# Infini-attention and GEGLU on one core: follow-up work placed by one table of step numbers, ten attention steps, last adds on VectorE

## The chip, the core and the metric

The kernel runs on one core of a Trainium2 chip. The metric is the device time of one execution in microseconds, as the median of several runs. The core has TensorE (PE) for matrix products, VectorE (DVE), ScalarE (ACT) and GpSimd (POOL) for the rest, SyncE (SP) which here only issues transfers, and 16 DMA engines. SBUF is the working memory, PSUM the memory that PE writes to.

## What is computed

The input x has 2048 rows of 448. It is layer-normed; the result xn goes through an attention with 16 heads of 28, and through a gated feed-forward of width 1792. The output is x + s * silu(b), s being the attention's result and b the feed-forward's.

```python
for s in range(4):                       # four segments of 512 rows
    qs, ks, vs = ...                     # 16 heads of 28
    p = softmax(qs @ ks.T * scale + causal mask)
    a_dot = p @ vs
    num, den = phi(qs) @ M, phi(qs) @ z + 1e-6    # phi(t) = t + 1 if t > 0 else exp(t)
    o = g * num / den + (1 - g) * a_dot           # g = sigmoid(beta), one per head
    M, z = M + phi(ks).T @ vs, z + sum(phi(ks))   # memory for the next segment
s = concat(o) @ wo
b = (gelu(xn @ w_gate) * (xn @ w_up)) @ w_down
out = x + s * silu(b)
```

## The kernel before

The work goes by the four segments. Each is held transposed (features on partitions, 512 rows along the free dimension), in four groups (G) of four heads, each head padded to 32 partitions. Two kinds of phases alternate on PE: gate 0, attention 0, gate 1, attention 1, gate 2, gate 3, attention 2, attention 3, tail. The order of instructions on every engine is the order in which the program calls them; nothing reorders them afterwards.

A **gate phase** (`gate_up`, L486) has 14 chunks. Each chunk takes eight matmuls (L496, and L503 on half the rows) into one of two PSUM buffers of `ps_s`; ACT applies GELU (L511), DVE multiplies gate by up (L512) and so frees the buffer. After every chunk the work that a table `steps` holds for this chunk number is called, then `tick()`.

An **attention phase** (`attention`, L577) has 12 steps: for each group the banks of `BANKS` (key block 0; key blocks 1 and 3 together; key block 2). A step makes the scores of four heads (L397, four matmuls side by side on 32 rows each) into both `ps_s` buffers, ACT takes the exponential of each (L403), GpSimd sets what lies above the diagonal to zero (L407), and two steps later PV (L418) sums into the one buffer of `ps_pv`. After a group's last bank `evac` (L426) copies the result to SBUF (L431) and sends its sums of weights, one row per head, by DMA to `dc` (L435). The PV of the last two steps is returned as two functions (`ends`) and called in the phase that follows. Between the steps stand fill units, in a merged order with an estimated cost each: projections of the next segment (`qk`, L314, cast at L318, then phi on ACT and DVE at L330, L337, L339; `v`, L352), the product with w_down (L523; tanh L526, L530) and the finish (L552, product L555, addition of x on GpSimd L559, store from GpSimd's queue L560). All of these use the three PSUM buffers of `ps_m`. `later(n, fn)` puts a function off by n ticks.

The **follow-up work** of a segment: `invert` (L444) turns the sums in `dc` into gate over sum, splits this into three bf16 terms and sends them by DMA to `rows`; a matmul with `spread` (L465) spreads them over the partitions of a group; `combine` (L472) scales the attention's result by them and adds the memory's. For the memory, `memory_read` (L439), an `invert` with side 1 and `scale_memory` (L468) do the same; `update` (L368) adds to M. Before, each of these is placed by hand: small tables made with `in_turn`, `tail` and `memory`, separately for each phase (L660 to L723).

`guard` (L204) checks on the chip that the weights are small enough for an exponential without a maximum: ACT squares wq and wk in four pieces, eight matmuls with a column of ones (L218) sum them, DVE does the rest. A second program (`general_path`) runs only if the check fails.

The **tail** finishes the w_down product of segment 3 (`d3[6:]`), runs the last two PV, inverts and combines group by group, and sums the product with wo in the freed `ps_s` buffers (L728). Then four output blocks go through two DVE or GpSimd operations each (L738, L740) to the output.

## Time and profile before

The median is 273.7 us (three runs, 271.87 to 273.88). The profiled execution took 273.37 us; its span in the trace is 271.6 us, all times below count from its start.

| engine | busy us | instructions |
|---|---|---|
| PE | 249.3 | 1630 |
| DVE | 190.0 | 371 |
| ACT | 155.5 | 226 |
| GpSimd | 100.2 | 203 |

| row of the page | operation | count, mean |
|---|---|---|
| L496, L503 | gate and up matmuls | 448, about 0.38 us each with overlap |
| L523 | w_down matmuls | 224 |
| L403 | exponential | 96, 885 ns |
| L407 | mask on GpSimd | 128, 449 ns |
| L512 | gate times up on DVE | 56, 685 ns |
| L559 | last add on GpSimd | 12, about 1.05 us |
| L560 | store issued from GpSimd | 12, 577 ns |
| L218 | sums of squares | 8, 352 ns |

The page's rows give, per line of the program, the busy time, the mean of one instruction and what ended the idle time before it. Matmuls overlap, so the distance between the starts of two of them is less than the duration of one. A timeline line gives the start, the time to the end of the group, the engine, line and tile, the number of instructions merged, and in brackets the idle time before it and what ended it.

### The profile page before, as it was taken

What the parts mean: (1) busy time and instruction counts of PE and PEld (TensorE: products, weight loads), DVE (VectorE), ACT (ScalarE), POOL (GpSimd) and SP (SyncE); (2) the same over time, 40 slices, a digit from 0 to 9 for tenths busy, and PEclk for the clock granted to TensorE, in tenths of its full rate; (3) what the DMA queues carried; (4) which work ended last, traced back from release to release, by engine and by line L of the source; (5) the groups of instructions that cost most, each with busy time, mean ns of one, the idle gap of its engine ahead of it and who ended that gap; (6) DMA issues with size and microseconds to landing.
All of it is one profiled execution on the core that took longest, in us unless ns stands there. A gap on an engine that the chain in (4) does not pass through costs nothing.

```text
span 271.6 us, 4546 instructions
## 1 busy us (share of the span) xinstructions
PE 249.3 (92%) x1630; PEld 104.5 (38%) x1630; DVE 190.0 (70%) x371; ACT 155.5 (57%) x226; POOL 100.2 (37%) x203
## 2 busy tenths in 40 slices
PE   7899999999999999999999999999899998995940
PEld 7543334433333335444434333344333333332410
DVE  5876977667686878577778646355878756876862
ACT  2546735788985335688963332625887687871100
POOL 2100410455521400966622205121776563658011
PEclk9999999999999999999999999999999999999795
DMA  7999026020110143101110310002000010001002
GB/s 221 393 277 213 0 41 154 12 23 19 23 22 6 34 85 113 22 18 39 40 37 0 63 24 0 4 6 72 18 21 21 5 29 8 4 1 57 19 7 75
DMA packets 26358, 15.11 MB, mean 56 GB/s; under 512 B 17880, under 2 KB 25048, under 8 KB 26328
## 3 DMA queue, kind: packets, MB, share of 16 engines
q1 hardware_dynamic: 23032, 9.96, 16.7%
q10 hardware_dynamic: 2720, 3.40, 3.9%
q0 software_dynamic: 576, 1.38, 1.5%
q8 instruction: 15, 0.25, 0.4%
q14 instruction: 15, 0.12, 0.2%
HBM read 9.18 MB, written 1.84 MB: 41 GB/s over the span
## 4 chain that ended last, share of the span: by engine, by line
PE 66%; DVE 16%; ACT 6%; DMA 5%; issue 3%; POOL 1%; SPq 1%; DVEq 0%; ACTq 0%
PE s L496 22%; PE m L523 11%; PE m L314 9%; PE s L503 5%; PE s L397 5%; PE m L352 4%; PE pv L418 3%; ACT pt L403 3%; PE m L465 2%; DMA x_sb<-in_A_x_dram 2%; PE m L552 2%; DVE hT L512 2%; DMA rows<-terms 2%; PE m L441 1%; DMA dc<-oU 1%
## 5 line engine op out<-in xcount | busy, mean ns | idle before, releaser
L403 ACT ACTIVATE pt<-s 128x1024 bf16<-128x1024 f32 (+1 forms) x96 | 79.2, 885 | 16.8 <-PE s L397 16.3
L407 POOL TENSOR_SCALAR_AFFINE_SELECT pt<-pt 128x256 bf16<-128x256 bf16 x128 | 54.6, 449 | 71.5 <-ACT pt L403 70.0
L511 ACT ACTIVATE gl<-s 128x512 bf16<-128x512 f32 x56 | 33.4, 597 | 55.5 <-PE s L496 28.7
L512 DVE TENSOR_TENSOR hT<-gl,s 128x512 bf16<-128x512 bf16 x56 | 38.4, 685 | 31.4 <-ACT gl L511 31.3
L523 PE MATMUL m<-wd_sb,hT 128*128 128x448 bf16 x224 | 52.3, 361 | 0.9 <-DVE wu_sb L470 0.9
L496 PE MATMUL s<-xnT,wg_sb 128*128 128x512 bf16 x168 | 45.7, 381 | 1.2 <-DVE hT L512 1.2
L496 PE MATMUL s<-xnT,wu_sb 128*128 128x512 bf16 x168 | 45.4, 379 | 0.0
L523 PEld LDWEIGHTS <-hT 128*128 128x128 bf16 x224 | 20.7, 99 | 23.6 <-issue 6.8
L496 PEld LDWEIGHTS <-wu_sb 128*128 128x128 bf16 x168 | 16.4, 98 | 19.8
L397 PE MATMUL s<-qT,kT 32*128 32x512 bf16 (+3 forms) x256 | 20.9, 301 | 2.6 <-ACT pt L403 2.3
L496 PEld LDWEIGHTS <-wg_sb 128*128 128x128 bf16 x168 | 14.1, 97 | 22.2 <-issue 9.7
L247 POOL TENSOR_TENSOR rstd<-rstd,nhalf 128x2 f32<-128x2 f32 x8 | 5.7, 712 | 45.7 <-DVE rstd L245 45.7
L503 PE MATMUL s<-xnT,wg_sb 64*128 64x512 bf16 x112 | 19.4, 384 | 0.4 <-DVE hT L512 0.4
L318 DVE CAST kT<-m 128x512 bf16<-128x512 f32 x16 | 11.0, 688 | 11.2 <-PE m L314 11.0
L418 PE MATMUL pv<-pt,vaug 128*32 128x512 bf16 (+3 forms) x256 | 17.3, 307 | 0.0
L314 PE MATMUL m<-xnT,wk_pad 128*128 128x512 bf16 x64 | 17.1, 380 | 0.0
L314 PE MATMUL m<-xnT,wq_pad 128*128 128x512 bf16 x64 | 16.8, 380 | 0.2 <-DVE vaug L354 0.2
L397 PEld LDWEIGHTS <-kT 32*128 32x128 bf16 x256 | 6.5, 91 | 23.4 <-issue 23.1
L526 ACT ACTIVATE th<-m 128x448 f32<-128x448 f32 x16 | 8.8, 548 | 11.3 <-PE m L523 11.1
L352 PE MATMUL m<-wv_sb,xnT 128*128 128x448 bf16 x64 | 14.1, 352 | 0.6 <-DVE wu_sb L431 0.3
L465 PE MATMUL m<-rows,spread 128*128 128x512 bf16 x28 | 11.0, 391 | 3.1 <-DMA rows<-terms 2.6
L431 DVE COPY oU<-pv 128x512 f32<-128x512 f32 x13 | 8.9, 688 | 4.8 <-PE pv L418 4.8
(102 smaller groups left out, 305.7 us busy)
## 6 DMA issues: line engine op xcount, KB each, us to landing
x_sb<-in_A_x_dram SPq DMA_DIRECT2D x7, 224.0 KB
wd_sb<-in_B_w_down_dram SPq DMA_DIRECT2D x1, 1568.0 KB
wg_sb<-in_B_w_gate_dram SPq DMA_DIRECT2D x1, 1344.0 KB
wu_sb<-in_B_w_up_dram ACTq DMA_DIRECT2D x1, 1344.0 KB
out_dram<-o_out POOLq DMA_DIRECT2D x12, 112.0 KB, 2.1
xr<-in_A_x_dram ACTq DMA_DIRECT2D x2, 448.0 KB
wo_sb<-in_A_wo_dram SPq DMA_DIRECT2D x4, 98.0 KB
dc<-oU SPq DMA_DIRECT2D x24, 8.0 KB
```

Source lines behind the costliest of these rows:

```text
L314: nc.tensor.matmul(out=pr[:], lhsT=wpad[nm][:, c, g * HG:(g + 1) * HG, :].rearrange("p h d -> p (h d)"), rhs=xnT[s][:, c, :], start=(c == ...
L352: nc.tensor.matmul(out=vp[:, 0:D], lhsT=xnT[s][:, c, b * P:(b + 1) * P], rhs=wv_sb[:, c, :], start=(c == 0), stop=(c == NDC - 1))
L397: nc.tensor.matmul(out=sp[i // 2][:, i % 2, c0:c0 + n], lhsT=kT[s][r, g, kb * P:(kb + 1) * P], rhs=qT[s][r, g, kb * P:L], start=True, stop ...
L403: nc.scalar.activation(out=pt[:, :, 0:w], in_=sp[pr][:, :, 0:w], func=ACT.Exp, scale=scale)
L407: nc.gpsimd.affine_select(out=v, in_=v, pattern=[[0, 2], [1, P]], compare_op=ALU.is_ge, fill=0.0, base=0, channel_multiplier=-1)
L418: nc.tensor.matmul(out=acc[i * HP:(i + 1) * HP, kb * P:L], lhsT=va[:, kb, g * HG + i, :], rhs=pts[i // 2][:, i % 2, c0:c0 + n], start=(kb ...
L465: nc.tensor.matmul(out=r[:], lhsT=spread[:, g, :], rhs=rows[side][:], start=True, stop=True)
L496: nc.tensor.matmul(out=gu[:, i, :], lhsT=w_sb[:, c, cols], rhs=xnT[s][:, c, :], start=start and c == 0, stop=stop and c == NDC - 2)
L503: nc.tensor.matmul(out=gu[:, i, :], lhsT=wg_sb[rs, NDC - 1, cols], rhs=xnT[s][rs, NDC - 1, :], start=start, stop=stop)
L511: nc.scalar.activation(out=gl[:], in_=gu[:, 0, :], func=ACT.Gelu_apprx_tanh)
L512: nc.vector.tensor_tensor(out=hT[s][:, fc, :], in0=gl[:], in1=gu[:, 1, :], op=ALU.mult)
L523: nc.tensor.matmul(out=d_ps[:, 0:D], lhsT=hT[s][:, fc, b * P:(b + 1) * P], rhs=wd_sb[:, fc, :], start=(fc == 0), stop=(fc == NFC - 1))
```

## The change

One dictionary, `PLAN`, now holds the step number of every piece of follow-up work. A single counter of slots runs through the whole program: 14 for each gate phase, 20 for each attention (two half steps for each of ten), then one for each unit of the tail. `put(name, fn)` files a function under its slot and asserts its order; `go()` is called once per slot and runs what is filed there. `merge` gives each list of fill units its own stretch of the phase (`"qk0": (0.609, 0.899)`), where it used to be the whole phase, or one of two parts of it.

Second, `STEPS` packs the key blocks of two groups into five steps, so that each step's exponential covers 512 columns for each head: block 2 of an odd group is computed with block 2 of the even group and kept until the odd group's accumulation has begun. `ptp` goes from 6 to 8 buffers, `pkp` from 3 to 2.

Third, the last add and its store go from GpSimd to DVE and SP; those of segment 2 write into `wq_pad`'s place. Three of segment 2's finish units move to the tail. The guard's squares are first added on GpSimd, so that two matmuls remain. `later` with 0 calls at once, the memory's product in `update` uses the buffers of `th`, and `follow` chooses the engine of the copies and inversions by phase. The aim is to keep PE supplied: fewer steps, fewer instructions on GpSimd, and each follow-up where its inputs are ready and its engine has room.

```diff
+PLAN = {
+    "stats10": 0, ..., "check0": 9, "check1": 3,
+    "check2": 8, "check3": 7, "check4": 13, "fill0": 9, "fill1": 1, "fill2": 18, "delay_phi": 2,
+    "delay_phi_end": 1, "delay_th": 0, "delay_sg": 2, "lead0": 2.29, "lead1": 1.56, "lead2": 2.93,
+    "lead3": 0.42, "upd0": (0.02, 0.233), "v0": (0.068, 0.299), "down0": (0.277, 1),
+    "qk0": (0.609, 0.899), "upd1": (0.072, 0.095), "v1": (0, 0.284), "down1": (0.319, 0.969),
+    "qk1": (0.122, 0.721), "fin1": (0.303, 1.05), "v2": (0.031, 1.05), "qk2": (0.082, 0.998),
+    "fin2": (0, 0.984), "down2": (0, 1.05), "split2": 8, "down3": (0.305, 1.05),
+    "fin3": (0.787, 1.05), "split3": 7, "fin_in": 1, "fin_at": 3, "end00": 34, "end01": 35,
+    "inv0": 36, ..., "inv2": 121,
+    "end30": 137, "end31": 137, "inv3": 138, "inv3l": 139, ..., "cmb30": 143, ..., "cmb31": 148,
+    ..., "cmb32": 150, ..., "scl32": 123, ..., "invm3": 112, "upd2": 89, "delay_out": 2, "check5": 17,
+}
...
-        ptp = pool("ptp", 6)
+        ptp = pool("ptp", 8)
...
-        pkp = pool("pkp", 3)
+        pkp = pool("pkp", 2)
...
+            for sq in sqs.values():
+                nc.gpsimd.tensor_tensor(out=sq[:, 0:2, :], in0=sq[:, 0:2, :], in1=sq[:, 2:4, :],
+                                        op=ALU.add)
+                nc.gpsimd.tensor_tensor(out=sq[:, 0, :], in0=sq[:, 0, :], in1=sq[:, 1, :], op=ALU.add)
...
-                for c in range(NDC):
-                    nc.tensor.matmul(out=np_[0:1, 0:D], lhsT=ones[:], rhs=sqs[nm][:, c, :],
-                                     start=(c == 0), stop=(c == NDC - 1))
+                nc.tensor.matmul(out=np_[0:1, 0:D], lhsT=ones[:], rhs=sqs[nm][:, 0, :],
+                                 start=True, stop=True)
...
-        BANKS = (((0, 0),), ((1, 0), (3, 384)), ((2, 0),))
+        STEPS = []
+        for a in range(0, G, 2):
+            b = a + 1
+            STEPS += [[(a, 0, 0)], [(a, 1, 0), (a, 3, 384)], [(a, 2, 0), (b, 2, 256)],
+                      [(b, 0, 0)], [(b, 1, 0), (b, 3, 384)]]
...
-                    nc.gpsimd.tensor_tensor(out=o_out[:], in0=t, in1=xr[s][:, b, :], op=ALU.add)
-                    nc.gpsimd.dma_start(out=o_v[s][:, b, :], in_=o_out[:])
-
-                later(99 if s == 2 else 1, rest)
+                    nc.vector.tensor_tensor(out=o_out, in0=t, in1=xr[s][:, b, :], op=ALU.add)
+                    nc.sync.dma_start(out=o_v[s][:, b, :], in_=o_out)
+
+                later(plan["delay_out"], rest)
...
-                    keyed.append(((c + u[0] / 2) / tot, n, u))
+                    keyed.append((a + (b - a) * (c + u[0] / 2) / tot, n, u))
...
+        def go():
+
+            for f in todo.pop(slot[0], ()):
+                f()
+            slot[0] += 1
...
+                    theirs.append((theirs or [lead])[-1] + 1.39)
...
-        ends = attention(3, d2[8:] + d3[:6] + finish_units(2), at, lead=0.6)
+        fin, w = finish_units(2), plan["fin_in"]
+        ends = attention(3, merge(3, down=d2[y:] + d3[:x], fin=fin[:w]))
+        gate_now[0] = True
+        follow(3, ends)
+        rest = d3[x:]
+        n = plan["fin_at"]
+        rest[n:n] = fin[w:]
+        for u in rest:
+            run([u])
+            go()
```

## The prediction

> **What bounds the kernel now.** I read the page's first part, then the windows cut by stage, then the timeline of one attention step and of the tail, and last the groups by form.
>
> ```profile
> PE 249.3 (92%) x1630; PEld 104.5 (38%) x1630; DVE 190.0 (70%) x371; ACT 155.5 (57%) x226; POOL 100.2 (37%) x203
> ```
>
> TensorE (PE) is the engine that is nearly always busy; so work taken off the others only counts where PE waits for it. The stages, by PE's own order: gate 0, attention 0, gate 1, attention 1, gates 2 and 3, attention 2, attention 3, the tail, the output.
>
> ```profile
> 24.20:45.60 21.40, 21.20 (x104) 8.21 (x104) 17.26 (x42) 9.92 (x15) 4.06 (x7) 1.00 0.34 57
> 45.60:76.20 30.60, 30.16 (x237) 12.72 (x236) 20.12 (x36) 26.05 (x38) 15.20 (x33) 1.00 0.18 34
> 76.20:103.40 27.20, 26.78 (x137) 10.04 (x135) 20.76 (x45) 12.63 (x22) 4.54 (x13) 1.00 0.24 47
> 103.40:136.00 32.60, 32.60 (x255) 14.19 (x254) 24.19 (x40) 26.25 (x36) 20.32 (x39) 1.00 0.15 39
> 136.00:187.10 51.10, 50.69 (x264) 20.00 (x263) 31.32 (x60) 20.96 (x35) 12.54 (x22) 1.00 0.09 18
> 187.10:217.00 29.90, 28.23 (x210) 10.87 (x208) 23.00 (x39) 24.06 (x31) 18.26 (x37) 1.00 0.10 30
> 217.00:243.00 26.00, 23.60 (x200) 9.23 (x200) 18.59 (x35) 21.04 (x28) 13.62 (x34) 1.00 0.05 11
> 243.00:262.50 19.50, 15.11 (x75) 6.25 (x75) 13.62 (x27) 2.47 (x5) 7.23 (x11) 0.91 0.09 26
> ```
>
> Columns: stretch, length, then busy PE, weight loads, DVE, ACT, POOL. PE waits visibly only in attention 2 (1.7 us), attention 3 (2.4) and the tail (4.4). Elsewhere its time goes down only if its work or its switching does. What switching costs is seen in one step of attention 0:
>
> ```profile
> 68.24 1.04 PE L314 MATMUL m<-xnT,wq_pad 128*128 128x512 bf16 x4
> 69.21 0.39 PE L397 MATMUL s<-qT,kT 32*128 32x512 bf16 x4
> 69.53 0.40 PE L418 MATMUL pv<-pt,vaug 128*32 128x384 bf16 x8
> 69.86 1.12 PE L523 MATMUL m<-wd_sb,hT 128*128 128x448 bf16 x5
> ```
>
> Four L314 take 1.04 us and elsewhere two take 0.60, so 0.22 us each; four need 0.88, but the next line starts after 0.97. The four score matmuls run side by side and need 0.22, but PV starts after 0.32; PV needs 0.22 and L523 starts after 0.33. Each change of shape (128*128, 32*128, 128*32) costs 0.1 us, 0.3 us a step.
>
> **What the Trainium skill says.** "TensorEngine Tiling (Array Packing)", Tiling Modes: changing the tiling mode drains TensorE. The 0.1 us above agrees. "SBUF — State Buffer", SBUF: two separate sides: a VectorE operation with two SBUF inputs and a GpSimd operation that reads SBUF exclude each other for a whole instruction. The trace fits: L339, two SBUF inputs, takes 692 ns beside idle GpSimd and 1024 ns on average in attention, where the masks (L407) run on GpSimd. "DMA: Bandwidth & Descriptors", Specifications: the first byte takes about 1 us through the GpSimd queue and 0.6 through Sync. No run here has the same store on both; through GpSimd's it lands in 2.1 us (the page). "VectorE: DVE Perf Modes", the errata section, prices an fp32 addition of two tensors at (N+151)/0.96 ns, 624 ns for N = 448.
>
> **The change, part by part.**
>
> *Guard.* In gate 0 the eight L218 matmuls hold PE from 35.93 to the next gate matmul at 37.54: 1.6 us. Four GpSimd adds now sum the squares first, and two matmuls remain, at table step 17, in attention 0. The adds are not in the trace; L559 (448 elements, 1.04 us) doubled for the 896 ones bounds them at 2 x (2.1 + 1.04) = 6.2 us on a GpSimd that is busy 4.1 of 21.4 us here. They can hold up DVE's scale_x (L251, L254), which feeds the next transposes; between nothing and a stall of 0.8, I take 0.3. Gate 0: -1.3. Attention 0 gains two matmuls at 0.19 and a switch: +0.5.
>
> *Ten steps.* Each attention loses two steps: 0.6 us of switching where PE sets the pace (attentions 0, 1, 2). Exp work:
>
> ```profile
> L403 ACT ACTIVATE pt<-s 128x1024 bf16<-128x1024 f32 x64 | 62.0, 1024 | 15.8 <-PE s L397 15.3 <-POOL pt L407 0.5
> L403 ACT ACTIVATE pt<-s 128x512 bf16<-128x512 f32 x32 | 17.6, 608 | 1.0 <-PE s L397 1.0
> ```
>
> Per attention, 16 x 1.024 + 8 x 0.608 = 21.2 us become 20 x 1.024 = 20.5: 0.77 less. In attention 3 PE has little other work and the loop scores, exp, scores sets the pace:
>
> ```profile
> 234.00 1.94 ACT L403 ACTIVATE pt<-s 128x1024 bf16<-128x1024 f32 x2 [0.52 <-PE s L397]
> 237.92 1.94 ACT L403 ACTIVATE pt<-s 128x1024 bf16<-128x1024 f32 x2 [0.56 <-PE s L397]
> ```
>
> ACT waits about 0.5 us for scores in a step. Two steps less: 2 x 0.52 + 0.77 = 1.8 us off attention 3.
>
> *The table.* Attention 0 takes the eight projections late (qk0, 0.609 to 0.899), so casts (688 ns), phi's two DVE operations (358 and 700 to 1024 ns) and the score copies press DVE in its second half: eight times about 1.9 us = 15 us, in some 15 us of PE time. I charge +0.5. Gate 1 has DVE-caused waits of PE (0.5 us at 90.13); the new order may remove them: -0.5. Attention 1 gives one more L465 to gate 1's spare DVE time: -0.3. Gates 2 and 3: PE waits at 140.65 (0.41) for the first product after the table load; projections end at 0.721 now, so no phi stands before that load: -0.5. Attention 3: the invert chain on DVE holds PE 0.87 us at 225.64; scl32 now stands three steps behind inv2: -0.9. The other placements (fills, reads, combines) I cost at nothing: the same instructions, beside gate matmuls that keep PE at 26.8 of 27.2 us.
>
> *Last adds on VectorE.* Twelve adds leave GpSimd. On DVE one costs 0.62 (the skill's price) to 1.03 us (L740 in the tail, beside GpSimd), so 7.5 to 12.4 us, nine of them in attention, where DVE is busy 74 to 77%. Behind each on DVE stand casts that free PE's three general PSUM buffers. GpSimd loses 12 x (1.05 + 0.56) us, which frees DVE's other two-input operations a little. I take 0.65 us each and that a tenth reaches PE, rounded down: +0.3; the ends are 0 and 6 (half of 12.4). The stores move behind Sync's other issues; each waits for its DVE add, as do the later ones: nothing.
>
> *Tail.* Before:
>
> ```profile
> 245.43 1.43 ACTq L457 DMA_DIRECT2D rows<-terms  x1
> 246.96 0.58 ACT L431 COPY oU<-pv 128x512 f32<-128x512 f32 x1 [3.62 <-DMA rows<-terms]
> 254.39 0.25 DVE L449 TENSOR_SCALAR dc<-dc,igate 32x64 f32<-32x64 f32 x1
> 259.68 0.38 PE L465 MATMUL m<-rows,spread 128*128 128x512 bf16 x1
> ```
>
> The last PV ends at T = 245.6; its copy sits 1.3 us behind an issue on ACT; the last group's inversion starts at T+8.8; wo ends at 262.5 = T+16.9. After: both ends at step 137, inversions at 138 and 139, and three finish units of segment 2 come into the tail. The inversion comes early, but DVE then carries: inv 2.4, two frees 1.1, inv 1.9, two products and three adds 3.1 (cmb30 starts at about T+8.5), each combine 1.3, and two sg operations, through which PE's three buffers turn. I get the last combine at T+16 and wo at T+16.6: -0.3.
>
> Sum: gate 0 -1.3; attention 0 -0.6 + 0.5 + 0.5 = +0.4; gate 1 -0.5; attention 1 -0.6 - 0.3 = -0.9; gates 2, 3 -0.5; attention 2 -0.6; attention 3 -1.8 - 0.9 = -2.7; adds +0.3; tail -0.3: in all -6.1. 273.7 - 6.1 = **267.6 us**.
>
> **Rivals.** (B) The placement removes almost every wait. Further than the sum: attention 2's remaining 1.7, gate waits 2, no charge for qk0, the guard adds and the adds (1.1), and a tail near its PE work (about 12 us for matmuls, plus combine and wo) 2.7 shorter: 7.5 more, 260.1 us. For it: PE's gaps are small and scattered, which placement can mend; against it: DVE's load rises. (C) Gains are eaten: adds at their upper end, +6.2 - 0.3 = 5.9 above the forecast: 273.5, no change. For it: DVE at 77% before the adds. (D) Slower: DVE becomes the bound: adds as in C, and the tail's DVE chain 3.5 us longer, because the moved finish units hold its buffers: 277.0. For it: my walk of the tail is DVE from T to T+16; against it: GpSimd contention falls.
>
> **How the numbers follow.** Forecast 0.49, B 0.27, C 0.13, D 0.11. The range runs from B, 260, to just short of C, 272.5; what is outside is D, half of C and a part of B below 260. Faster by over 1% (below 271): forecast and B, 0.76; within 1%: C, 0.13; slower: D, 0.11.
>
> **What would show it.** Right: gate 0 near 20 us with no guard matmul; attention 3 near 23.5; 80 exp instructions of 1024; the adds on DVE at 0.62 to 0.75; the last spread matmul near T+15. Wrong: PE waits for DVE in attentions 0 to 2 beyond 2 us in all; adds near 1 us; the tail longer than 17 us after the last PV.

## The result, and the profile after

The changed kernel takes **265.39 us** (median of four runs, 265.22 to 266.45) against 273.79 us for the kernel before, run on the same chip at the same time (four runs, 271.87 to 274.49). The ratio is 0.9712, 95% interval 0.9657 to 0.9767: 8.4 us faster. The forecast was 267.6 us, with a range of 260.0 to 272.5, so the direction, the range and the likeliest case were right. Several of its terms were not: two stages came out about 2 us longer than forecast and two about 2 us shorter, so that the sum came near the measurement partly by luck.

The profiled execution took 266.45 us with a span of 264.7 us, about 1.1 us more than the other three executions (spans 263.5 to 263.6). Where that microsecond lies is shown in the last section. The page's first part for the changed kernel:

```profile
PE 244.9 (93%) x1624; PEld 102.5 (39%) x1624; DVE 192.3 (73%) x383; ACT 154.5 (58%) x210; POOL 88.8 (34%) x183
```

TensorE is still the engine that sets the pace. It is busy for 4.4 us less, although only six short matmuls are gone (1624 against 1630): the trace counts much of what passes between two overlapping matmuls as busy, and a stretch at half clock too. VectorE took over twelve additions and is hardly busier (192.3 against 190.0 us). The windows, cut at the changed kernel's own stage boundaries (gate 0, attention 0, gate 1, attention 1, gates 2 and 3, attention 2, attention 3, tail), with the same columns as before:

```profile
26.70:46.70 20.00, 19.62 (x96) 7.68 (x96) 16.09 (x36) 9.97 (x16) 7.34 (x7) 1.00 0.19 44
46.70:76.00 29.30, 29.12 (x235) 12.41 (x234) 20.27 (x40) 25.69 (x34) 13.02 (x31) 1.00 0.15 35
76.00:103.10 27.10, 27.10 (x141) 9.98 (x139) 21.16 (x46) 12.99 (x23) 5.69 (x15) 1.00 0.16 29
103.10:135.30 32.20, 31.92 (x250) 14.01 (x249) 25.84 (x46) 26.48 (x33) 15.92 (x33) 1.00 0.23 59
135.30:187.70 52.40, 51.08 (x269) 19.83 (x267) 32.36 (x60) 20.42 (x34) 11.54 (x20) 1.00 0.08 16
187.70:214.40 26.70, 26.36 (x205) 10.39 (x203) 23.66 (x46) 23.23 (x27) 12.84 (x29) 1.00 0.12 35
214.40:239.80 25.40, 24.52 (x217) 9.35 (x217) 16.84 (x32) 21.38 (x25) 15.23 (x36) 1.00 0.06 15
239.80:255.50 15.70, 12.64 (x66) 5.76 (x62) 13.77 (x31) 2.16 (x4) 0.00 (x0) 1.00 0.09 26
```

Attention 2 waited 1.7 us of its length before and waits 0.34 now. The tail's clock is 1.00 where it was 0.90 to 0.91. Gates 2 and 3 have got longer: 1.3 us of them are idle on PE. The same stages from start to start follow, read from the matmuls themselves. A stage ends where PE starts the first matmul of the next; "start" ends where the third chunk of gate 0 begins, and T is the end of the last PV:

| stage | before | after | difference | forecast |
|---|---|---|---|---|
| start | 24.16 | 26.71 | +2.55 | 0 |
| gate 0 | 21.47 | 20.03 | -1.44 | -1.3 |
| attention 0 | 30.64 | 29.30 | -1.34 | +0.4 |
| gate 1 | 27.13 | 27.06 | -0.07 | -0.5 |
| attention 1 | 32.78 | 32.24 | -0.54 | -0.9 |
| gates 2, 3 | 50.94 | 52.38 | +1.44 | -0.5 |
| attention 2 | 29.89 | 26.72 | -3.17 | -0.6 |
| attention 3, to T | 28.63 | 25.39 | -3.24 | -2.7 |
| tail, T to the end of wo | 16.85 | 15.64 | -1.21 | -0.3 |
| output, from there to the end of the span | 9.15 | 9.25 | +0.1 | 0 |
| last adds, over all stages | | | (in the rows) | +0.3 |
| sum | 271.6 | 264.7 | -6.9 | -6.1 |

These are the two profiled executions. The changed kernel's was the longest of its four, by the 1.1 us named above, which the last section places in the start; so the medians differ by 8.4 us and the traces by 6.9. Two rows belong together: nine matmuls of 128x448, about 0.20 us apart and so about 1.8 us of PE, have moved from attention 3 into the tail (three finish units moved there, three w_down matmuls the other way). The two stages together went from 45.5 to 41.0 us.

The groups by form show the two operations that the change altered in kind:

```profile
L445 ACT ACTIVATE pt<-s 128x1024 bf16<-128x1024 f32 x80 | 77.5, 1023 | 12.9 <-PE s L439 9.7 <-POOL pt L449 2.7
L616 DVE TENSOR_TENSOR o_out<-sg,xr 128x448 bf16<-128x448 f32 x8 | 5.4, 677 | 0.0
L616 DVE TENSOR_TENSOR wq_pad<-sg,x_sb 128x448 bf16<-128x448 f32 x4 | 2.4, 616 | 0.0
```

The 96 exponentials of two widths have become 80 of one, and ScalarE waits 9.7 us for scores before them, where it waited 16.3. An addition on VectorE takes 616 to 677 ns.

From the timeline of the changed kernel's tail (T is 239.83):

```profile
245.25 0.38 PE L514 MATMUL m<-rows,spread 128*128 128x512 bf16 x1 [1.19 <-DVE sg L611]
247.25 0.68 DVE L533 TENSOR_TENSOR oU<-oU,m 128x512 f32<-128x512 f32 x1
252.66 0.38 PE L514 MATMUL m<-rows,spread 128*128 128x512 bf16 x1
254.54 0.93 PE L836 MATMUL s<-wo_sb,oT 128*128 128x448 bf16 x4 [1.51 <-DVE oT L534]
```

The wait of 1.51 us before the last product stands in both kernels. Apart from it the longest wait of PE is 1.19 us, where it was 2.61 us; the first combine starts at T+7.4 and the last spread matmul at T+12.8.

### The profile page after: what moved, and what is told of

It reads as the page before. It is cut to its first block, busy times and chain, and to the rows that moved or that the text cites. A ratio compares the mean times of both kernels' runs of the same rounds, so it can differ in the third digit from the quotient of the medians.

```text
span 264.7 us, 4500 instructions
## 1 busy us (share of the span) xinstructions
PE 244.9 (93%) x1624; PEld 102.5 (39%) x1624; DVE 192.3 (73%) x383; ACT 154.5 (58%) x210; POOL 88.8 (34%) x183
## 4 chain that ended last, share of the span: by engine, by line
PE 71%; DVE 16%; ACT 5%; issue 2%; DMA 2%; POOL 1%; POOLq 0%
PE s L547 25%; PE m L573 12%; PE m L348 10%; PE s L554 6%; PE s L439 4%; PE m L387 4%; PE pv L458 4%; PE m L608 2%; ACT pt L445 2%; DVE hT L563 2%; DVE oU L533 2%; PE m L514 2%; DVE xn L285 1%; DVE oT L534 1%; ACT gl L562 1%
## 5 line engine op out<-in xcount | busy, mean ns | idle before, releaser
L445 ACT ACTIVATE pt<-s 128x1024 bf16<-128x1024 f32 x80 | 77.5, 1023 | 12.9 <-PE s L439 9.7
L449 POOL TENSOR_SCALAR_AFFINE_SELECT pt<-pt 128x256 bf16<-128x256 bf16 x128 | 56.6, 462 | 66.1 <-ACT pt L445 63.2
L573 PE MATMUL m<-wd_sb,hT 128*128 128x448 bf16 x224 | 50.2, 353 | 0.0
L439 PE MATMUL s<-qT,kT 32*128 32x512 bf16 (+3 forms) x256 | 19.1, 300 | 1.1 <-ACT pt L445 0.5
L348 PE MATMUL m<-xnT,wq_pad 128*128 128x512 bf16 x64 | 17.5, 380 | 0.0
L387 PE MATMUL m<-wv_sb,xnT 128*128 128x448 bf16 x64 | 15.9, 386 | 0.2 <-DVE vaug L389 0.2
L458 PE MATMUL pv<-pt,vaug 128*32 128x128 bf16 (+3 forms) x256 | 15.8, 306 | 0.0
L554 PEld LDWEIGHTS <-wg_sb 64*128 64x128 bf16 x112 | 5.3, 93 | 19.1 <-issue 18.5
L439 PEld LDWEIGHTS <-kT 32*128 32x128 bf16 x256 | 5.5, 91 | 18.5 <-issue 18.3
L608 PE MATMUL m<-wo_sb,oT 128*128 128x448 bf16 x48 | 11.4, 353 | 0.4 <-DVE sg L611 0.2
```

Source lines behind the costliest of these rows:

```text
L348: nc.tensor.matmul(out=pr[:], lhsT=wpad[nm][:, c, g * HG:(g + 1) * HG, :].rearrange("p h d -> p (h d)"), rhs=xnT[s][:, c, :], start=(c == ...
L387: nc.tensor.matmul(out=vp[:, 0:D], lhsT=xnT[s][:, c, b * P:(b + 1) * P], rhs=wv_sb[:, c, :], start=(c == 0), stop=(c == NDC - 1))
L439: nc.tensor.matmul(out=sp[i // 2][:, i % 2, c0:c0 + n], lhsT=kT[s][r, g, kb * P:(kb + 1) * P], rhs=qT[s][r, g, kb * P:L], start=True, stop ...
L445: nc.scalar.activation(out=pt[:, :, 0:w], in_=sp[pr][:, :, 0:w], func=ACT.Exp, scale=scale)
L449: nc.gpsimd.affine_select(out=v, in_=v, pattern=[[0, 2], [1, P]], compare_op=ALU.is_ge, fill=0.0, base=0, channel_multiplier=-1)
L458: nc.tensor.matmul(out=acc[i * HP:(i + 1) * HP, kb * P:L], lhsT=vaug[s % 2][:, kb, g * HG + i, :], rhs=pts[i // 2][:, i % 2, c0:c0 + n], s ...
```

## The experiments

The theory after the result: the ten steps and the table are worth something mainly together; the last adds help at the place where GpSimd had held VectorE; and the two stages that got longer (start, gates 2 and 3) are the price of single entries of the table. The experiments split the change into its parts first and then mend the two losses. Comparisons of stages are safer here than those of totals: a stage that an edit does not touch agrees to 0.1 us from trace to trace, while start and output do not.

### Ten steps alone

The kernel before with only the packing of the key blocks; the hand-made tables keep their places, step numbers inside an attention taken times 20/24.

```diff
-        ptp = pool("ptp", 6)
+        ptp = pool("ptp", 8)
...
-        pkp = pool("pkp", 3)
+        pkp = pool("pkp", 2)
...
-        BANKS = (((0, 0),), ((1, 0), (3, 384)), ((2, 0),))
...
+        STEPS = []
+        for a in range(0, G, 2):
+            b = a + 1
+            STEPS += [[(a, 0, 0)], [(a, 1, 0), (a, 3, 384)], [(a, 2, 0), (b, 2, 256)],
+                      [(b, 0, 0)], [(b, 1, 0), (b, 3, 384)]]
...
+                at.setdefault(k * 20 // 24, []).extend(fs)
```

> The kernel before, with the ten packed steps alone (hand tables kept, their slots in attention scaled from 24 to 20; eight pt buffers, two pkT buffers). Theory of the prediction: each step saved is worth 0.3 us of switching in attentions 0 to 2 (30.7, 32.6 and 29.9 us become 30.1, 32.0 and 29.3) and a turnaround of 0.5 us plus 0.77 us of exp in attention 3 (from its first scores to the end of the last PV 28.6 us becomes 26.8): 3.6 us in all, so about 270. Rival 1 (packing explains attention 2 as well): attention 2 falls by 2 us or more, to 28 or less, and the time to 268.5 or less. Rival 2 (the packing is worth nothing without the table): no attention falls by more than 0.4 us, the time stays within 1 us of before.

Measured: 276.3 us, ratio 1.0087 (1.0056 to 1.0118), a little slower than before; none of the three cases written down foresaw that. Attention 0 takes 28.99 us (1.65 less) and attention 2 28.34 (1.55 less). But attention 1 takes 34.30 (1.52 more), attention 3 31.48 (2.85 more) and the tail 18.13 (1.28 more). The timeline of this kernel shows at which waits:

```profile
122.36 0.68 DVE L318 CAST qT<-m 128x512 bf16<-128x512 f32 x1
123.09 1.02 PE L314 MATMUL m<-xnT,wk_pad 128*128 128x512 bf16 x4 [0.85 <-DVE qT L318]
...
224.68 0.38 PE L466 MATMUL m<-rows,spread 128*128 128x512 bf16 x1 [1.89 <-DVE wu_sb L471]
...
252.47 0.59 PE L466 MATMUL m<-rows,spread 128*128 128x512 bf16 x1 [4.42 <-DMA rows<-terms]
```

All three are follow-up work at a place that no longer fits: a cast behind phi's operations on VectorE, the scaling of the memory behind the inversion of segment 2 (0.87 us in the kernel before), and the last segment's inversion, which arrives 4.42 us late in the tail (2.61 before). PE's waits grow by 1.7 us in attention 1 and by 1.2 us in attention 3. The other 1.6 us of attention 3 fit a stretch of 3.41 us at half clock that follows the wait of 1.89 us (last section). What follows: the packing itself saves 1.6 us in attentions 0 and 2, and all of it is lost again with these hand tables at scaled places. Hand tables made anew for ten steps were not tried.

### The table with the old twelve steps

The other half: the changed kernel with the old steps put back; every entry of the table inside or behind an attention is moved by 24/20. The adds and the guard stay changed.

```diff
-        for a in range(0, G, 2):
-            b = a + 1
-            STEPS += [[(a, 0, 0)], [(a, 1, 0), (a, 3, 384)], [(a, 2, 0), (b, 2, 256)],
-                      [(b, 0, 0)], [(b, 1, 0), (b, 3, 384)]]
+        for a in range(G):
+            STEPS += [[(a, 0, 0)], [(a, 1, 0), (a, 3, 384)], [(a, 2, 0)]]
...
```

> The changed kernel with the old twelve steps in each attention (every table entry inside or behind an attention moved by 24/20 to the same place), everything else as changed. It does alone what the table, the guard and the adds do, without the packing; the ten steps alone (the kernel before plus the packing) had given 276.3. Theory T (packing saves about 1.6 us in attentions 0 and 2, as it did alone, and what it lost alone in attention 1, attention 3 and the tail was old placement that no longer fitted): 265.4 + 4 x 1.5 = 271.4 (270 to 272.5), each attention 1.0 to 2.0 us longer than in the changed kernel. Rival R1 (the packing is worth nothing here either, the table gives it all): 264.5 to 266. Rival R2 (only both together help): 273 or more.

Measured: 273.3 us, ratio 0.9984 (0.9936 to 1.0031): no measurable difference from the kernel before. Rival R2 came true. The theory's amount was too small: each attention is 0.85 to 2.8 us longer than in the changed kernel (31.63, 33.09, 29.05 and 28.15 us). Together with the previous run this makes a square:

| ratio to the kernel before | work placed by hand | table, guard and adds as changed |
|---|---|---|
| twelve steps | 1 | 0.9984 (0.9936 to 1.0031) |
| ten steps | 1.0087 (1.0056 to 1.0118) | 0.9712 (0.9657 to 0.9767) |

Neither half gains, both together gain 2.9%. The right-hand column holds the adds and the guard as well; the adds alone gain 0.5% on the kernel before (next section), so the table by itself gives the twelve steps nothing. One limit remains: each placement was made for the steps of its own kernel and only scaled to the other's, and one made anew might do better; that was not tried. So the square shows that table and ten steps fit each other, not that no table could help the twelve or no hand placement the ten.

### The last adds alone, on both kernels

```diff
-                    nc.gpsimd.tensor_tensor(out=o_out[:], in0=t, in1=xr[s][:, b, :], op=ALU.add)
-                    nc.gpsimd.dma_start(out=o_v[s][:, b, :], in_=o_out[:])
+                    nc.vector.tensor_tensor(out=o_out[:], in0=t, in1=xr[s][:, b, :], op=ALU.add)
+                    nc.sync.dma_start(out=o_v[s][:, b, :], in_=o_out[:])
```

On the kernel before:

> The kernel before, with the last adds on VectorE and their stores from Sync alone. Theory of the prediction: the adds take 0.62 to 0.75 us each on VectorE and reach TensorE hardly: time within 0.5 us of before (273.5 to 274.3), attention 2 at 29.9 plus or minus 0.3. Rival 1 (the relief of GpSimd is what shortened attention 2): attention 2 falls by 1.5 us or more, the time to 272 or less. Rival 2 (VectorE cannot take them without a new placement): attentions 1 and 2 grow by 0.5 us or more each, the time to 275 or more.

Measured: 272.69 us, ratio 0.9954 (0.9937 to 0.9970), 1.3 us faster, which none of the cases written down had. And the opposite edit on the changed kernel, adds and stores back on GpSimd:

> The kernel after, with the last adds and their stores back on GpSimd. Theory of the prediction: the adds on VectorE were worth about nothing; the time is within 0.5 us of the kernel after (265.4), attention 2 stays at 26.7 plus or minus 0.3. Rival 1 (relief of GpSimd): attention 2 grows by 1.5 us or more and the time to 267 or more. Rival 2 (VectorE was near its limit): the time falls below 264.9.

Measured: 266.64 us (266.62 to 267.53), 1.25 us above the changed kernel's 265.39. As ratios to the kernel before, these two are 0.9746 (0.9709 to 0.9783) and 0.9712 (0.9657 to 0.9767), so their intervals overlap. From the end of the start to the end of wo the adds gain 1.8 us on the kernel before (238.3 to 236.5) and 0.6 us on the changed one (229.4 to 228.8); the other 0.6 of the second pair's 1.25 us is not in these stages. So the adds **gained**, where the forecast charged 0.3, and less in the changed kernel than the totals say.

In the attentions the forecast's charge is found: on the kernel before, attention 2 takes 30.27 us with the adds on VectorE and 29.89 without, on the changed one 26.72 and 26.47; the other three agree to 0.1 us. The gain is in the tail, 14.62 us instead of 16.85 on the kernel before, 15.64 instead of 16.46 on the changed one. The timeline of the kernel before around its T of 245.64:

```profile
244.17 0.74 DVE L454 CAST terms<-dc 96x64 bf16<-96x64 f32 x1
...
245.43 1.45 DVE L456 TENSOR_TENSOR dc<-dc,terms 96x64 f32<-96x64 f32 x1
245.74 1.04 POOL L559 TENSOR_TENSOR o_out<-sg,x_sb 128x448 bf16<-128x448 f32 x1
...
249.30 0.38 PE L465 MATMUL m<-rows,spread 128*128 128x512 bf16 x1 [2.61 <-DMA rows<-terms]
```

And the same operations with the adds on VectorE (T is 246.34):

```profile
244.87 0.19 DVE L454 CAST terms<-dc 96x64 bf16<-96x64 f32 x1
...
245.58 0.22 DVE L456 TENSOR_TENSOR dc<-dc,terms 96x64 f32<-96x64 f32 x1
...
248.20 0.38 PE L465 MATMUL m<-rows,spread 128*128 128x512 bf16 x1 [0.81 <-DVE o_out L559]
```

Two small operations of the inversion took 0.74 and 1.45 us beside GpSimd's additions, and 0.19 and 0.22 without them. That is 1.8 us on the chain to which PE's longest wait in the tail belongs, and that wait falls from 2.61 to 0.81 us. On the changed kernel, with the adds back on GpSimd, the inversion's first operation is held for 1.05 us, where it takes 0.25, and PE then waits behind it:

```profile
237.95 1.03 POOL L616 TENSOR_TENSOR wq_pad<-sg,x_sb 128x448 bf16<-128x448 f32 x1
237.99 1.05 DVE L495 TENSOR_SCALAR dc<-dc,igate 96x64 f32<-96x64 f32 x1 [1.34 <-DMA dc<-oU]
...
241.39 0.92 PE L608 MATMUL m<-wo_sb,oT 128*128 128x448 bf16 x4 [0.98 <-DVE sg L611]
```

It is the lock that the Trainium skill describes ("SBUF — State Buffer", SBUF: two separate sides), which covers one-input operations in some of VectorE's modes as well as those with two inputs. The trace agrees with it, and shows the amount: the held operation ends 0.05 to 0.1 us behind GpSimd's addition, even the one of 1.45 us, whose record begins 0.3 us ahead of that addition. On the kernel before, the tail's 2.23 us are made up in another way than this alone. PE's waits in it fall by only 0.6 us in all (from 4.33 to 3.72), since it waits longer later. The other 1.6 are its busy time, 12.51 and 10.93 us in the windows, at a granted clock of 0.90 and 1.00: with the long wait went a stretch at half clock (last section).

### The guard's sums alone

Four GpSimd additions and two matmuls in place of eight, still inside gate 0 of the kernel before.

```diff
+            for sq in sqs.values():
+                nc.gpsimd.tensor_tensor(out=sq[:, 0:2, :], in0=sq[:, 0:2, :], in1=sq[:, 2:4, :],
+                                        op=ALU.add)
+                nc.gpsimd.tensor_tensor(out=sq[:, 0, :], in0=sq[:, 0, :], in1=sq[:, 1, :], op=ALU.add)
...
-                for c in range(NDC):
-                    nc.tensor.matmul(out=np_[0:1, 0:D], lhsT=ones[:], rhs=sqs[nm][:, c, :],
-                                     start=(c == 0), stop=(c == NDC - 1))
+                nc.tensor.matmul(out=np_[0:1, 0:D], lhsT=ones[:], rhs=sqs[nm][:, 0, :],
+                                 start=True, stop=True)
```

> The kernel before, with the guard's squares summed on GpSimd and two matmuls in place of eight, still in gate 0. Theory of the prediction: six matmuls of 0.19 us less on TensorE, against up to 0.3 us from GpSimd holding VectorE: gate 0 (21.5 us from its third chunk to the first v matmul) becomes 20.4 to 20.7, the time falls by about 0.9 us. Rival (GpSimd's adds hold VectorE's scaling of the next segment for long): gate 0 stays at 21.3 or more.

Measured: 274.74 us, ratio 1.0029 (1.0008 to 1.0049): not faster, rather slower, as the rival had it. Gate 0 takes 22.32 us, 0.85 more, although six matmuls are gone. Its timeline:

```profile
32.48 1.88 POOL L215 TENSOR_TENSOR pqT<-pqT 128x896 bf16<-128x896 bf16 x1
32.50 1.89 DVE L258 TENSOR_SCALAR xn<-x_sb,mv,rstd 128x64 bf16<-128x64 bf16 x1
...
35.04 0.81 PE L500 MATMUL s<-xnT,wg_sb 128*128 128x512 bf16 x3 [0.88 <-DVE hT L516]
...
43.38 0.81 PE L500 MATMUL s<-xnT,wg_sb 128*128 128x512 bf16 x3 [0.94 <-DVE hT L516]
```

A `scale_x` (VectorE's scaling of a block of rows in the layer norm, in two instructions of 448 and 64 columns; a turn is this and the transposition after it) lasts for its 64 columns, 0.28 us when alone, as long as the GpSimd addition that it meets (1.89 beside 1.88 us). The product `hT` stands behind it on VectorE, and PE waits 0.88 us for the product. The second wait, 0.94 us, stands behind the work that is late by then on VectorE, the guard's own reductions and a `scale_x` held by the mask fill among it. The two, 1.82 us, are more than what the matmuls free (they hold PE for 0.66 us instead of 1.61): 0.87 us lost, as measured. In the changed kernel the same additions stand at other steps, with the last part in attention 0 and the mask fill gone from gate 0, and cost one wait of 0.37 us. What the fill has to do with it, the next run shows.

### The mask fill back in gate 0

The changed kernel runs `fill_masks`, with GpSimd's memset and three affine selects, at step 1, so at the very start. Here it is put at step 12.

```diff
-    ... "fill1": 1, ...
+    ... "fill1": 12, ...
```

At the start of the changed kernel the selects hold `scale_x`, 0.29 us when alone:

```profile
9.28 0.79 DVE L285 TENSOR_SCALAR xn<-x_sb,mv,rstd 128x64 bf16<-128x64 bf16 x1
9.30 2.43 POOL L183 TENSOR_SCALAR_AFFINE_SELECT spread<-spread 128x512 bf16<-128x512 bf16 x3
```

> The changed kernel with the table entry of the mask fill (fill1) at step 12 instead of 1. Theory (the GpSimd memset and affine selects of the fill, run at 8.7 to 11.7 us, hold VectorE's scale_x of the first layer norm by 0.4 to 0.9 us and so the start): scale_x there back to 0.4 and 0.3 us, the third gate-0 chunk starts at 24.2 to 25.0 instead of 26.7, total 263.9 (263.2 to 264.6); the selects then run in gate 0, which loses at most 0.5. Rival (the late start is only the lower TensorE clock that this execution was granted at the start, whatever GpSimd does): 265.4 +- 0.5.

Measured: 265.9 us, ratio 0.9701 (0.9672 to 0.9730): no change in the total, as the rival had it, but two changes inside. The start ends at 24.47, as the theory had it and as in the kernel before (24.16). But gate 0 takes 21.37 us instead of 20.03, where at most 0.5 was expected. Its timeline:

```profile
41.62 1.90 POOL L242 TENSOR_TENSOR xr<-xr 128x896 bf16<-128x896 bf16 x1
41.72 1.85 DVE L285 TENSOR_SCALAR xn<-x_sb,mv,rstd 128x64 bf16<-128x64 bf16 x1
...
44.21 0.39 PE L554 MATMUL s<-xnT,wg_sb 64*128 64x512 bf16 x2 [1.47 <-DVE hT L563]
```

The selects push the guard's additions back until they meet the last `scale_x`. So the fill at the start was a trade: it costs the start about 1.1 us (last section) and spares gate 0 1.3 us.

### The mask fill cut in two

The fill's GpSimd part moves to attention 0, where there is no `scale_x`; VectorE's part stays at step 1.

```diff
-            nc.gpsimd.memset(spread[:], 0.0)
+
+        def fill_spread(n):
+            if n == 0:
+                nc.gpsimd.memset(spread[:], 0.0)
+                return
...
-            for t in range(3):
+            for t in (n - 1,):
...
+    ... "fill3": 20, "fill4": 23, "fill5": 26, "fill6": 29, ...
```

> The changed kernel with the mask fill cut in two: VectorE's part stays at step 1, GpSimd's memset and three affine selects go one by one to steps 20, 23, 26 and 29, in attention 0, where no scale_x runs. Theory (these GpSimd operations cost something exactly where a scale_x runs beside them, at the start or in gate 0): the third gate-0 chunk starts at 24.2 to 24.6 as in the kernel before, gate 0 takes 20.0 to 20.2, attention 0 at most 0.4 more than 29.30, total 263.5 (262.9 to 264.3). Rival (in attention 0 they hold up the masks and so PV): attention 0 takes 30.3 or more, total 265 or more.

Measured: 264.87 us, ratio 0.9660 (0.9628 to 0.9692). The stages are as the theory had them: the start ends at 24.37, gate 0 takes 20.03, attention 0 29.55 (0.25 more). The total is 0.5 us below the changed kernel's and so outside the 262.9 to 264.3 that was expected. The changed kernel's usual start ends near 25.5 and not at 26.7 (last section), so only 0.9 us were to be had; and the output, from the end of wo to the end of the span, took 9.6 us here and 9.25 there. In the fourteen profiled executions it lies between 9.15 and 10.15 us. Up to the end of VectorE's last addition it takes 4.0 us in every one; the spread lies behind that, where only the last stores are under way (5.15 to 6.15 us), without a pattern in the edits that I can see. It stays unexplained, and totals can differ by it where the stages agree.

### Segment 1's combine additions on VectorE, and both first mends

Gates 2 and 3 contain one wait of PE of 1.29 us for `hT`, before the last chunk of gate 2. Beside it, two of segment 1's combines add on GpSimd for 1.27 us each and hold the last turn's `scale_x` (0.96 and 1.24 us):

```profile
156.97 2.52 POOL L534 TENSOR_TENSOR oT<-oU,oU 128x512 bf16<-128x512 f32 x2 [1.91 <-DVE oU L533]
157.40 0.96 DVE L282 TENSOR_SCALAR xn<-x_sb,mv,rstd 128x448 bf16<-128x448 bf16 x1
158.29 1.24 DVE L285 TENSOR_SCALAR xn<-x_sb,mv,rstd 128x64 bf16<-128x64 bf16 x1
159.44 1.27 DVE L563 TENSOR_TENSOR hT<-gl,s 128x512 bf16<-128x512 bf16 x2
160.17 0.39 PE L554 MATMUL s<-xnT,wg_sb 64*128 64x512 bf16 x2 [1.29 <-DVE hT L563]
```

Here these additions go to VectorE.

```diff
-                add = nc.gpsimd if s == 1 else nc.vector
+                add = nc.vector
```

> The changed kernel with segment 1's four combine additions on VectorE instead of GpSimd. Theory (two of these additions, 1.27 us each on GpSimd at step 78, hold VectorE's scale_x of the same step at 1.0 and 1.2 us, and with it the product that PE waits 1.29 us for): gates 2 and 3 take 51.0 to 51.4 instead of 52.4, total 264.3 (263.8 to 264.8). Rival (VectorE has the additions' 4 x 0.7 us on top and PE waits for it elsewhere in the gates): gates 2 and 3 at 52.0 or more, total 265.4 +- 0.5.

Measured: 267.84 us, ratio 0.9772 (0.9735 to 0.9809): 2.4 us above the changed kernel. The wait at the end of gate 2 stayed at 1.21 us. The `scale_x` did fall to 0.39 and 0.29 us, but two additions of 0.69 us now take VectorE's time in the same step. So taking the lock away alone did not end the wait: other work stands in its place. And attention 2 took 27.93 us instead of 26.72, which neither theory had. The rival was right on the gates, and wrong on the total. The rest of the 2.4 us is outside the stages (0.6 us in the output); two of the four executions took 267.0 to 267.2 us and two 268.5.

With the late fill of the run above as well:

> Both mends at once: the mask fill at step 12 and segment 1's combine additions on VectorE. If both theories hold the gains add, since they lie in different stages: 262.8 (262.0 to 263.6), faster than the changed kernel. If only one holds, 264 to 264.5; if none, 265.4.

Measured: 266.92 us, ratio 0.9743 (0.9713 to 0.9774); gate 0 again 21.35, gates 2 and 3 52.30, attention 2 27.94: neither mend holds, which is worse than the "none" that was written down.

Why attention 2 got longer is seen on ScalarE. With the additions on VectorE:

```profile
188.14 0.60 ACT L562 ACTIVATE gl<-s 128x512 bf16<-128x512 f32 x1 [1.66 <-PE s L547]
190.26 1.28 ACT L445 ACT_TABLE_LOAD   x1 [1.53 <-PE s L439]
191.56 1.94 ACT L445 ACTIVATE pt<-s 128x1024 bf16<-128x1024 f32 x2
```

ScalarE loads the table for the exponential before attention 2's first one, 1.28 us. Here the load waits for PE's scores; in the changed kernel it starts 0.42 us after the last gelu and before the scores:

```profile
188.94 1.28 ACT L445 ACT_TABLE_LOAD   x1 [0.42 <-issue]
```

To test that this is the whole loss, the next kernel has the additions on VectorE and one exponential of a single column, thrown away, right after the last gelu:

```diff
...
+                if s == 3 and fc == NFC - 1:
+                    nc.scalar.activation(out=warm[:], in_=nhalf[:, 0:1], func=ACT.Exp)
```

> The kernel with segment 1's combine additions on VectorE (267.84), plus one exponential of 128x1 on ScalarE, thrown away, right after gate 3's last gelu. In that kernel attention 2 took 27.93 instead of 26.72 us and ScalarE's table load stood behind PE's first scores (it started at 190.26, 1.5 us after the last gelu, and not 0.4 us after it). Theory (that late table load is the whole loss of attention 2): the load starts within 0.5 us of the last gelu, attention 2 takes 26.6 to 27.0, total 266.7 (266.2 to 267.2). Rival (the additions on VectorE cost attention 2 in another way): attention 2 stays at 27.9, total 267.8.

Measured: 266.39 us, ratio 0.9709 (0.9673 to 0.9745). The load starts behind the gelu:

```profile
187.12 1.28 ACT L565 ACT_TABLE_LOAD   x1
188.42 0.20 ACT L565 ACTIVATE warm<-nhalf 128x1 f32<-128x1 f32 x1
188.65 1.94 ACT L445 ACTIVATE pt<-s 128x1024 bf16<-128x1024 f32 x2
```

Attention 2 is back at 26.84 us and the total 1.45 us below that of the additions on VectorE alone. So the late load was 1.1 of the 1.2 us that attention 2 had lost. The total is still 1.0 us above the changed kernel's, with the stages from gate 0 to the end of wo alike to 0.12 us; 0.8 us of it is in the profiled execution's output. Both programs with the additions on VectorE and no early exponential have the late load, and none of the other twelve; why the load carries the wait for the scores there, though the edit is elsewhere, stays open.

### The combines apart

If not the engine, then the crowd: at step 78 the table has two combines and a turn, with another turn at 77. Here the combines go to steps of their own.

```diff
-    ... "cmb10": 78, "cmb11": 80, "cmb12": 78, "cmb13": 81, ...
+    ... "cmb10": 79, "cmb11": 82, "cmb12": 83, "cmb13": 81, ...
```

> The changed kernel with segment 1's combines moved from steps 78, 80, 78, 81 to 79, 82, 83, 81, so that none shares a step with the last two turns (77 and 78). The mend by another engine had left PE's wait of 1.2 us in gate 3 where it was. Theory (what is too much at step 78 is two combines and a turn at once, on whichever engine the additions run): that wait falls to 0.5 us or less, gates 2 and 3 take 51.2 to 51.7 instead of 52.4, total 264.5 (264.0 to 265.0). Rival (the work only moves, PE waits as long at another step): gates 2 and 3 at 52.1 or more, total 265.4 +- 0.5.

Measured: 264.84 us, ratio 0.9651 (0.9622 to 0.9681). Gates 2 and 3 fall from 52.38 to 51.41. The wait at the end of gate 2 (the recorded text places it in gate 3) is gone; the longest that is left is one of 0.44 us, two chunks earlier. No addition of GpSimd now stands beside the last turn:

```profile
155.02 0.39 DVE L282 TENSOR_SCALAR xn<-x_sb,mv,rstd 128x448 bf16<-128x448 bf16 x1
155.32 0.29 DVE L285 TENSOR_SCALAR xn<-x_sb,mv,rstd 128x64 bf16<-128x64 bf16 x1
```

The theory holds in the stage, which it had at 51.2 to 51.7. The total lies in its range too, but by the total alone the gain could not be told from the spread: the ratio's interval overlaps with the changed kernel's.

### Both mends that hold

The fill cut in two and the combines apart.

> Both of these: the fill cut in two, and segment 1's combines apart. The two lie in different stages, so the gains should add: 262.6 (261.9 to 263.5), faster than the changed kernel by about 1%. If one of the two fails, 263.5 to 264.5; if both, 265.4.

Measured: 264.1 us (263.28 to 264.69), ratio 0.9632 (0.9600 to 0.9664): the fastest of all. The stages are those of the two single runs: start 24.21, gate 0 20.03, attention 0 29.55, gates 2 and 3 51.41, attention 2 26.72, attention 3 25.39. So both mends hold, and their gains add in the stages. The profiled execution, 263.28 us, lies in the expected 261.9 to 263.5; the median of the four does not and would by itself read as one mend failing. It is 1.3 us below the changed kernel; the intervals of the two ratios just overlap.

## Why the prediction was right, and where it was not

**The main mechanism, ten steps.** Right in direction, too small in size for attentions 0 and 2. The forecast took 0.6 us per attention, six changes of shape at 0.1. The number of changes is right (34 to 28 in attention 0 with the packing alone), but the stage lost 1.65 us. Adding the distances from each group of matmuls to the next in attention 0, the scores fall from 4.59 to 3.61 us and PV from 3.01 to 2.56, here with four matmuls fewer, which moved into gate 1. The 16 score matmuls with 256 columns took 1.99 us in four groups of four, and 0.78 in two groups of eight. The failed step is the one that read the price of a step from a step of full width. The narrow step cost more: in three of its four groups the second pair of matmuls starts 0.3 to 0.5 us after the first, when an exponential has freed the second score buffer, and the timeline merges the four into one line.

**Attention 0, +0.4, measured -1.34.** Besides the packing, the charges fail: +0.5 for the guard's matmuls and +0.5 for late projections. With the packing alone the stage takes 28.99 us, in the changed kernel 29.30. Both charges, with all else that the table moved here, come to 0.31 us. The "eight times about 1.9 us = 15 us, in some 15 us of PE time" was a load on VectorE, and PE waited for VectorE for only 0.18 us in this stage. (The 1024 ns in that load is the mean of the eight L339 for the keys; the twelve for the queries took 754 ns.)

**Attention 2, -0.6, measured -3.17.** The largest miss. Of the 1.7 us that PE waited, the forecast expected nothing to go, though its rival B did. The waits fall to 0.34 us. The square's runs say where the rest comes from: the packing alone gives 1.55, the table with adds and guard alone 0.84, both 3.17 us. So the table there gives more with the ten steps than with the twelve.

**Attention 3, -2.7, measured -3.24.** Right in sum, by luck. The forecast gave 1.8 us to the steps and 0.9 to the table, as if each came by itself. Alone the steps cost 2.85 us more, and alone the table gains 0.48. And about 1.8 of the 3.24 us is PE's work that moved into the tail; PE's waits fell by 1.5 us (2.40 to 0.88). The sign "attention 3 near 23.5" was counted on a window that ends 2.6 us before T; carried to T it is 25.9, measured 25.39.

**Attention 1, -0.9, measured -0.54; gate 1, -0.5, measured -0.07.** Mis-sized. Attention 1 takes 1.52 us more with the steps alone and 0.31 more with the table alone, so its gain too comes only from both. In gate 1 the wait of 0.42 us is gone, but four more PV matmuls and one more spread matmul now run there.

**Gate 0, -1.3, measured -1.44.** The number is right, the reason only half. The 1.6 us are saved, but the forecast's bound for the contention, "between nothing and a stall of 0.8", was too low: in gate 0 of the kernel before the same additions cost waits of 1.82 us. The changed kernel comes off with 0.37 because other entries of the table moved with it, the fill above all (a wait of 1.47 us when it is put back).

**Start, 0, measured +2.55; gates 2 and 3, -0.5, measured +1.44.** The failed step is the sentence that cost the other placements, "fills, reads, combines", at nothing because PE is busy beside them. PE was busy, but VectorE's order was not free: a fill beside a `scale_x` and two combines beside a turn each made PE wait. Two counter-tests show it: 1.0 us back in gates 2 and 3, and 2.3 us at the start, of which 1.1 is the fill itself and 1.2 the clock of that one execution. In gates 2 and 3 the forecast's own mechanism came true, the wait of 0.41 us at 140.65 is gone. Of the other 0.5 us that stay, four more PV matmuls and one more spread matmul are a part.

**Adds, +0.3, measured -1.8 in the stages of the kernel before and -0.6 in those of the changed one.** The duration (0.62 to 0.68 us) was right and the cost in attention 2 (0.25 to 0.38 us) near; the sign of the sum was wrong. (A tenth of twelve times 0.65 us is 0.8, not 0.3; it was rounded down a long way.) The forecast asked what the adds would hold up on VectorE. It mentioned that GpSimd's release "frees DVE's other operations a little" and did not look for where such an operation stands on PE's path: the inversion in the tail.

**Tail, -0.3, measured -1.21.** The order was walked rightly, but the last spread matmul comes at T+12.8 instead of the expected T+15 and the last combine with it. The walk let each wait follow from VectorE's chain; what it left out is PE's clock, 1.00 instead of 0.90. The sum works out from the traces: about 1.8 us of matmuls came in, PE's waits fell by 1.3 us (4.38 to 3.04), and the stretch at half clock, worth about 1.7 us (estimate, last section), is gone.

As for the signs named ahead: gate 0 near 20 us without guard matmuls, 80 exponentials, adds at 0.62 to 0.75 us on average and PE waiting for VectorE for 0.8 us in attentions 0 to 2 were all seen. Rivals C (adds near 1 us each) and D (VectorE the bound) are refuted by the adds' own runs. Rival B, that the placement removes nearly all waits, is what happened in attention 2. Its sum was too large: "gate waits 2" is more than the 1.0 us that the three gate windows show, which the forecast had already taken; and its tail, 3.0 us shorter in all, fell by 1.21. Even with the losses at the start and in gate 2 mended the kernel takes 264.1 us, not 260.1.

## What to carry to other kernels

When a change shortens the steps of a pipeline and also moves what hangs between them, do not add up two separate gains: here neither gained alone (ratios 1.0087 and 0.9984) and both gave 2.9%. For every GpSimd instruction that is moved, look up which VectorE instructions stand beside it at the old and at the new place; the price is up to the whole GpSimd instruction, paid by whatever waits behind the held one. And a placement beside a busy PE is free only if the engine that frees PE's buffers has room in that very step.

## What the runs showed of the hardware that was not expected

**A wait of PE can be paid twice, and whether it is depends on a grid in time.** In all fourteen traces the stretches at one clock last whole multiples of 3.413 us, up to the last change: 245.76, 3.41 and 10.24 us in the kernel before (72, 1 and 3 times), 6.83 and 3.41 us at the changed kernel's start (2 and 1). So the clock changes on a grid, and the grid lies differently in each execution. Two windows of it in the tail of the kernel before, with most of the wait of 2.61 us in the first (the granted clock is the third figure from the end of each line):

```profile
247.54:250.95 3.41, 1.44 (x7) 0.70 (x8) 1.29 (x3) 0.45 (x2) 2.77 (x5) 1.00 0.21 73
250.95:254.36 3.41, 3.36 (x10) 1.15 (x9) 3.34 (x6) 0.00 (x0) 0.53 (x1) 0.50 0.10 34
```

PE is busy for 1.44 us of the first, and runs the whole second one at half clock. Its 3.36 us of work there would take half of that at full clock, so the wait costs about another 1.7 us (estimate). Two windows of the changed kernel's start, where GpSimd's fill holds `scale_x`:

```profile
7.88:11.29 3.41, 1.61 (x14) 0.87 (x14) 2.83 (x8) 2.22 (x4) 3.09 (x5) 1.00 1.02 400
11.29:14.70 3.41, 3.41 (x11) 1.42 (x10) 2.16 (x6) 0.59 (x1) 0.45 (x1) 0.50 1.04 355
```

Cut on its own grid, every trace says the same: the clock fell behind each of the twenty windows in which PE was busy for up to 1.61 us, and behind no other window at full clock, the least busy of which had 1.64 us. (The trace models the ends of matmuls, so this limit is not exact to hundredths.) The ten steps alone fell twice, after waits of 1.89 and 4.42 us. The Trainium skill ("TensorE: Matmul & The Clock Gate", Part 1: The HAM clock gate) says that the clock follows how busy PE has been in a window of about 3.4 us; these traces agree with the length. It lets the clock fall after an idle window; here a window that was 47% busy was enough.

In six profiled kernels the fill stands at step 1. Two have a start window under the limit (1.61 and 1.43 us) and end the start at 26.7 and 27.0 us. The least busy start windows of the other four have 2.0 to 2.5 us, and their start ends at 25.4 to 25.5. The eight without the fill there, the kernel before included, end it at 24.2 to 24.5. So the fill itself costs 1.1 us, and the lowered clock another 1.2 in some executions. Where the grid cuts the gaps matters: with the adds back on GpSimd the start has a stretch of 3.41 us in which PE is busy for 1.58, but the grid divides it, no window is below 2.01, and the clock stays. In the same way the tail of the adds alone had no window below 1.89 us, though another grid could have caught 1.51. In the changed kernel's tail no stretch of 3.41 us has PE busy for less than 1.74 us, wherever the grid lies.

**A table load can carry its activation's wait.** The same load of 1.28 us began 1.5 us after the last gelu in two programs and 0.42 us after it in most others. One small activation of the right function, put where the old table is last used, brought 1.1 us of attention 2 back for 0.2 us of ScalarE.
